# A six-layer cross network on one core: the second half's remainder columns turned by VectorE, one block of products moved, x0 read in twelve pieces, the last layer opened with narrow matmuls

## The chip, the cores and the metric

The kernel runs on one NeuronCore of a Trainium2 chip. TensorE multiplies matrices (its result goes to PSUM, eight banks), ScalarE evicts PSUM and adds biases, VectorE multiplies and adds elementwise, POOL (GpSimd) makes small copies, and SP issues DMA transfers; ScalarE's queue can issue transfers too. Every engine works through its own queue in order and waits on semaphores. The metric is the device time of one execution in microseconds (us); the median of three runs counts.

## The reference

```python
B, F, D, L = 4096, 26, 16, 6
Din = min(F * D, 1024)          # 416
x0: [4096, 416]   ws: [6, 416, 416]   bs: [6, 416]      # all bf16

def reference(x0, ws, bs):
    x = x0
    for l in range(ws.shape[0]):
        x = x0 * (x @ ws[l] + bs[l]) + x
    return x
```

Each layer is a product with a 416 x 416 matrix, a bias, a product with the input x0 and a sum with the layer's own input.

## The kernel before

**Layout.** For layers 0 to 4 the activations lie transposed: features on the partitions, rows of the batch as columns. 416 features are three full blocks of 128 (`NK = 3`, tiles `XM`) and a remainder of 32 (`R`, tiles `XR`). The 4096 rows are two halves `s` of 2048, each of four groups `g` of 512 (`CW`). The remainder of one half is packed: group `g`'s 32 features lie on partitions 32g to 32g+31, so `XR` holds 512 columns for each half. `XM[0]`, `XR[0]` are x0; the layers write `XM[1]`, `XM[2]` by turns. `XRd` is x0's remainder with the upper and lower 64 partitions exchanged.

**Loading (lines 92 to 125).** SP's queue issues eight transposing transfers that bring x0's full blocks, one for each half and group (L75), and between the fifth and the sixth the second half's remainder, `load_xrem1` (L84); then the weights of layer 1 (L71), the remainder rows of the weights (L90), the other layers' weights, x0 row by row in four transfers (`X0rows`, L123; only the last layer reads it) and the last bias (L125). ScalarE's queue issues the first layer's weights, the biases, the first half's remainder in four transfers into `xrig` (`load_xrem0`, L80) and the first layer's remainder rows, and then copies the latter to other partitions (L108). POOL fills a block-diagonal copy of the remainder weights (`fill_wd`, L129) and, between, rearranges `xrem` into `xrig[:, 1]` (L132).

**The first layer (`first_layer`, called for both halves).** Full-width products (L212) go into PSUM tiles of two banks, the remainder's row products (L219) are row-tiled: four matmuls of 32 rows side by side in the array. `x0_rem(s, tpr)` turns x0's remainder: four TensorE transposes (L155) into PSUM, then three VectorE copies (L158), one to `XR[0]` and two to `XRd`. For `s = 0` it stands in the middle of the first products; for `s = 1` at the end of the first half, behind the remainder products `mm_rem` (L191 and L196, column-tiled: 32 columns of the array for each group) and ahead of the second block's elementwise work. `ew_main` is that work for 1024 columns: ScalarE adds the bias out of PSUM (L163), VectorE multiplies by x0 (L164) and adds the layer's input (L167). PSUM is one pool of four two-bank tiles, taken by turns: a new tile waits until ScalarE has emptied the oldest. The buffers `t` between ScalarE and VectorE are six.

**Layers 1 to 4 (lines 280 to 311).** Six tiles (half, block) in three pairs `n = 0, 2, 4`. In each pair, tile a gets its full products in column-tiled form (`mm_full`, L179: four matmuls of 32 columns side by side) and then its row products (L185), tile b its row products and then its full ones. Behind the first pair, `rem_pair` computes both halves' remainder products (L191, L196), their eviction (L171) and their elementwise work (L172, L173). These write the remainder that the next layer reads in its row products. In layer 4 the results also go, by transposing transfers, to `XLrows` (L203).

**The last layer (lines 313 to 380).** Its output has batch rows on the partitions: weights are the activations, 128 columns of them at a time, and the moving side is the weight matrix, 416 wide. Four rounds of eight banks each. `mm_q_full` (L325) makes three full-width matmuls for one bank; in each round `done` banks open with them (two in the first round), then `mm_q_rem` adds the remainder (L331) and the bias (L334) by row-tiled matmuls, and the others close with them. ScalarE copies out of PSUM (L352), VectorE multiplies by `X0rows` (L353) and adds `XLrows` (L342), and SP stores (L343).

**Order.** A planner orders each engine's queue by estimated times, within the data's dependences; an instruction handed to `keep_in_program_order` stays where the program has it among its engine's instructions. Transfers get one of eight semaphores each, by turns in the planner's order.

Of the kernel before, what the change touches and what calls it, by code (L numbers as in the profile page):

```python
# [11 lines left out]
BF16 = mybir.dt.bfloat16  # L12
# [4 lines left out]
def kernel(  # L17
# [7 lines left out]
    nc = tc.nc  # L25
    B, D = x0.shape
    L = ws.shape[0]
    P = 128
    NK = 3
    R = D - NK * P  # L30
    assert R == 32 and B == 4096 and D == 416 and L >= 2
    NS = 2
    NG = 4
    CW = 512
    SW = NG * CW
    NBT = B // P
# [3 lines left out]
    big = ctx.enter_context(tc.tile_pool(name="big", bufs=1))  # L40
# [4 lines left out]
    x0_v = x0.rearrange("(bt p) d -> p bt d", p=P)  # L45
    out_v = out.rearrange("(bt p) d -> p bt d", p=P)

    ident = const.tile([P, P], BF16)
    dz = const.tile([P, 2], FP32)
    ones = const.tile([P, P], BF16)  # L50
    WM = const.tile([P, L, NK, D], BF16)
# [6 lines left out]
    X0rows = big.tile([P, NBT, D], BF16)  # L58
    XLrows = big.tile([P, NBT, D], BF16)
    scrR = [big.tile([P, 4, P], BF16, name=f"scrR{s}") for s in range(NS)]  # L60
    xrem = big.tile([P, 16, R], BF16)
    xrig = big.tile([P, NS, 4, P], BF16)
    XRd = big.tile([P, NS * CW], BF16)
    XM = [big.tile([P, NK, B], BF16, name=f"XM{i}") for i in range(3)]
    XR = [big.tile([P, NS * CW], BF16, name=f"XR{i}") for i in range(3)]

    def col0(s, g):
        return SW * s + CW * g

    def load_wm(eng, l):  # L70
        eng.dma_start(WM[:, l], ws[l, 0:NK * P, :].rearrange("(k p) n -> p k n", p=P))  # L71

    def load_x0t(s, g):
        c0 = col0(s, g)
        nc.sync.dma_start_transpose(out=XM[0][:, :, c0:c0 + CW], in_=x0[c0:c0 + CW, 0:NK * P])  # L75

    def load_xrem0():
        with nc.allow_non_contiguous_dma(reason="64B row segments"):
            for i in range(4):
                nc.scalar.dma_start(xrig[:, 0, i, :].rearrange("p (g r) -> p g r", g=NG), x0_v[:, i:16:4, NK * P:D])  # L80

    def load_xrem1():
        with nc.allow_non_contiguous_dma(reason="64B row segments"):
            nc.sync.dma_start(xrem[:], x0_v[:, 16:32, NK * P:D])  # L84

    def load_wr0():
        nc.scalar.dma_start(WR[0:R, 0, :], ws[0, NK * P:D, :])
# [17 lines left out]
    for g in range(1, NG):  # L105
        dst, src = WR[32 * g:32 * g + 32, 0, :], WR[0:R, 0, :]
# [4 lines left out]
    for g in range(2, NG):  # L111
        load_x0t(0, g)
    load_x0t(1, 0)
    load_xrem1()
    for g in range(1, NG):
        load_x0t(1, g)
    load_wm(nc.sync, 1)
# [1 line left out]
        load_wr(nc.sync, g, 1, L)  # L119
    for l in range(2, L):  # L120
        load_wm(nc.sync, l)
    for q in range(4):
        nc.sync.dma_start(X0rows[:, 8 * q:8 * q + 8, :], x0_v[:, 8 * q:8 * q + 8, :])  # L123
    for g in range(NG):
        nc.sync.dma_start(bLr[32 * g:32 * g + 1, :], bs[LL:LL + 1, :])  # L125

    def fill_wd(l0, l1):
        for g in range(NG):
            nc.gpsimd.tensor_copy(WD[32 * g:32 * g + 32, l0:l1, g, :], WR[32 * g:32 * g + 32, l0:l1, NK * P:D])  # L129

    fill_wd(0, 1)
    nc.gpsimd.tensor_copy(xrig[:, 1].rearrange("p i (g r) -> p i g r", g=NG), xrem[:].rearrange("p (g i) r -> p i g r", g=NG))  # L132
    fill_wd(1, L)

    wps = psum.tile([P, CW], FP32, tag="ps", name="wps")
# [14 lines left out]
        nc.vector.tensor_copy(bM[:], pb[:, 0:NK, 0:L])  # L150
        nc.vector.tensor_copy(bR[:], pb[:, 3, 0:L])

    def x0_rem(s, tpr):
        for i in range(4):
            nc.tensor.transpose(tpr[:, 128 * i:128 * i + 128], xrig[:, s, i, :], ident[:])  # L155
        for dst, src in ((slice(0, P), slice(0, P)), (slice(64, P), slice(0, 64)), (slice(0, 64), slice(64, P))):
            to = XR[0] if dst == src else XRd
            nc.vector.tensor_copy(to[dst, CW * s:CW * s + CW], tpr[src])  # L158

    def ew_main(l, s, m, h, pt, cur, nxt, pin=False):  # L160
        c0 = col0(s, 2 * h)
# [37 lines left out]
    def new_pts():  # L199
        return [psum.tile([P, 2, CW], FP32, tag="ps", name=f"pt{h}") for h in range(2)]  # L200

    def xl_dmat(s, k, nxt):
        nc.sync.dma_start_transpose(out=XLrows[:, 16 * s:16 * s + 16, 128 * k:128 * k + 128],  # L203
                                    in_=nxt[:, k, SW * s:SW * s + SW])

    def first_layer(s):
        cur, curR, nxt, nxtR = XM[0], XR[0], XM[1], XR[1]

        def full(pt, m, h, gl, after_row):
            c0 = col0(s, 2 * h + gl)  # L210
            for k in range(NK):
                nc.tensor.matmul(pt[:, gl, :], lhsT=WM[:, 0, k, 128 * m:128 * m + 128], rhs=cur[:, k, c0:c0 + CW],  # L212
                                 start=(k == 0 and not after_row), stop=(k == NK - 1 and after_row))

        def row(pt, m, h, opens):
            for gl in range(2):
                rg = 32 * ((2 * h + gl) ^ (2 if m == 1 else 0))
                src = XRd if m == 1 else curR
                nc.tensor.matmul(pt[:, gl, :], lhsT=WR[rg:rg + 32, 0, 128 * m:128 * m + 128],  # L219
                                 rhs=src[rg:rg + 32, CW * s:CW * s + CW],  # L220
                                 start=opens, stop=not opens, tile_position=(rg, 0))

        def ph(m):
            return psum.tile([P, 2, CW], FP32, tag="ps", name=f"ph{m}")

        pa = [ph(m) for m in range(NK)]
        if s == 0:
            for m in range(NK):
                full(pa[m], m, 0, 0, False)
            tp0 = psum.tile([P, CW], BF16, tag="ps", name="tpr")  # L230
            x0_rem(0, tp0[:])
            for m in range(NK):
                full(pa[m], m, 0, 1, False)
        else:
            for m in range(NK):
                for gl in range(2):
                    full(pa[m], m, 0, gl, False)
        pb = [ph(0)]
        row(pa[0], 0, 0, False)
        row(pb[0], 0, 1, True)  # L240
        row(pa[2], 2, 0, False)
        row(pa[1], 1, 0, False)
        for m in range(NK):
            ew_main(0, s, m, 0, pa[m], cur, nxt)
        for m in range(NK):
            if m:
                pb.append(ph(m))
            for gl in range(2):
                full(pb[m], m, 1, gl, m == 0)
        row(pb[1], 1, 1, False)  # L250
        row(pb[2], 2, 1, False)
        pr = psum.tile([P, 2, CW], FP32, tag="ps", name="pr")
        mm_rem(0, s, pr[:, 0, :], cur, curR)
        if s == 0:
            x0_rem(1, pr[:, 1, :].bitcast(BF16)[:, 0:CW])
        for m in range(NK):
            ew_main(0, s, m, 1, pb[m], cur, nxt, pin=(s == 0))
        ew_rem(0, s, pr[:, 0, :], curR, nxtR)
# [20 lines left out]
    cur, curR = XM[1], XR[1]  # L279
    for l in range(1, LL):  # L280
        nxt, nxtR = XM[1 + (l % 2)], XR[1 + (l % 2)]
        feeds_last = (l == LL - 1)
        tiles = [(s, m) for s in range(NS) for m in range(NK)]
        pts = {}

        def finish(t):
            s, m = t
            for h in range(2):
                ew_main(l, s, m, h, pts[t][h], cur, nxt)
            if feeds_last:  # L290
                xl_dmat(s, m, nxt)

        for n in range(0, len(tiles), 2):
            ta, tb = tiles[n], tiles[n + 1]
            pts[ta] = new_pts()
            for g in range(NG):
                mm_full(l, ta[0], ta[1], g, pts[ta], cur, True, False)
            mm_row(l, ta[0], ta[1], pts[ta], curR, False, True)
            pts[tb] = new_pts()
            mm_row(l, tb[0], tb[1], pts[tb], curR, True, False)  # L300
            if feeds_last and n == 4:
                xl_rem(0)
            finish(ta)
            for g in range(NG):
                mm_full(l, tb[0], tb[1], g, pts[tb], cur, False, True)
            finish(tb)
            if n == 0:
                rem_pair(l, cur, curR, nxtR, feeds_last)
        if feeds_last:
            xl_rem(1)  # L310
        cur, curR = nxt, nxtR

    l = LL
# [4 lines left out]
    def q_cols(q, g):  # L318
        s, i = quads[q]
        c = col0(s, g) + 128 * i  # L320
        return slice(c, c + 128)

    def mm_q_full(q, g, py, closes):
        for k in range(NK):
            nc.tensor.matmul(py[:, 0:D], lhsT=cur[:, k, q_cols(q, g)], rhs=WM[:, l, k, :],  # L325
                             start=((not closes) and k == 0), stop=(closes and k == NK - 1))
# [34 lines left out]
    for q, at, done in rounds:  # L361
        tiles = [psum.tile([P, 2, CW], FP32, tag="ps", name=f"py{n}") for n in range(4)]
        bank = [tiles[n][:, a, :] for n, a in at]

        def close(u, n):
            tl, a = at[u]
            ew(q + u // 4, u % 4, n, tiles[tl][:, a:a + n, 0:D], nc.scalar if q + 2 == NQ and u == 7 else nc.sync)

        for u in range(done):
            mm_q_full(q, u, bank[u], False)  # L370
        mm_q_rem(q, bank[0:4], done)
        close(0, done)
        mm_q_rem(q + 1, bank[4:8], 0)
        for u in range(done, 8):
            mm_q_full(q + u // 4, u % 4, bank[u], True)
            if at is not PAIRS:
                close(u, 1)
            elif u % 2:
                close(u - 1, 2)
# [31 lines left out]
```

## Time and profile before

| | us |
|---|---|
| runs (median of 3; lowest to highest) | 130.45; 130.38 to 130.53 |
| the profiled execution | 130.58 |
| its span, first to last instruction | 128.8 |
| granted TensorE clock | 1.00 |

| Stretch of the span, us | what runs | TensorE busy | VectorE busy | ScalarE busy |
|---|---|---|---|---|
| 0 to 5.9 | first loads | 5.13 | 0.06 | 0.00 |
| 5.9 to 26.8 | first layer | 20.90 | 15.31 | 14.70 |
| 26.8 to 46.1 | layer 1 | 19.30 | 18.42 | 14.24 |
| 46.1 to 65.4 | layer 2 | 19.30 | 17.39 | 13.72 |
| 65.4 to 84.6 | layer 3 | 19.20 | 17.29 | 13.62 |
| 84.6 to 103.7 | layer 4 | 19.10 | 17.20 | 14.14 |
| 103.7 to 115.7 | last layer, up to the last round's remainder | 12.00 | 10.95 | 8.55 |
| 115.7 to 128.8 | end | 8.71 | 10.06 | 7.91 |

A line of the profile names the line of the kernel (L212 is line 212), the engine (PE is TensorE's matmuls, PEld its weight loads, DVE is VectorE, ACT ScalarE; ACTq and SPq are the sequencers), the operation, and the tiles as out<-in. In the chain of waits the columns are start, duration and what ran; in the timeline they are start, duration and the instruction with its count, and in brackets the engine's idle time before it and what ended that.

### The profile page before, as it was taken

The numbers are of one execution on the slowest core, as the hardware profiler recorded it, in microseconds if no ns is written. First come the engines' busy times: TensorE is split into PE (matmuls) and PEld (weight loads), VectorE is DVE, ScalarE is ACT, GpSimd is POOL, SyncE is SP. The second block draws the span as 40 slices with busy tenths as digits, with TensorE's granted clock in tenths as the row PEclk, the third lists the DMA queues.
The fourth block names the chain that finished last, engine by engine and source line by source line (L and its number), as shares of the span: only waits on it lengthen the run. The fifth ranks groups of instructions, "written<-read, shape, count | busy, mean of one in ns | idle before, by whom it ended". The sixth has DMA issues, their size and how long they took to land.

```text
span 128.8 us, 3973 instructions
## 1 busy us (share of the span) xinstructions
PE 123.6 (96%) x1691; PEld 55.1 (43%) x1691; DVE 106.7 (83%) x195; ACT 86.9 (67%) x99; POOL 6.2 (5%) x18
## 2 busy tenths in 40 slices
PE   7999999999999999999999999999999999999960
PEld 3343443344545444434444544444444445445420
DVE  0023989999999898989898989898989899898991
ACT  0138873887848667848668848668858896569670
POOL 4004300600000000000000000000000000000000
PEclk9999999999999999999999999999999999999999
DMA  4999999999990000000000000000297999985754
GB/s 95 244 231 207 163 153 264 253 328 333 336 291 9 5 0 8 0 0 5 0 5 0 5 0 5 0 5 0 45 163 169 119 237 191 217 261 186 235 178 138
DMA packets 42102, 16.37 MB, mean 127 GB/s; under 512 B 30906, under 2 KB 42084, under 8 KB 42084
## 3 DMA queue, kind: packets, MB, share of 16 engines
q1 hardware_dynamic: 39368, 15.53, 53.9%
q10 hardware_dynamic: 2716, 0.59, 2.5%
q8 instruction: 13, 0.21, 0.7%
q14 instruction: 5, 0.04, 0.1%
HBM read 6.15 MB, written 3.41 MB: 74 GB/s over the span
## 4 chain that ended last, share of the span: by engine, by line
PE 89%; DVE 6%; issue 2%; ACT 1%; DVEq 0%
PE pt L179 49%; PE ph L212 13%; PE py L325 8%; PE pt L185 5%; PE pr L196 5%; PE wps L139 4%; DVE t L353 4%; DVE o L342 2%; PE pr L191 2%; PE ph L219 1%; PE py L331 1%; PE py L334 1%; ACT t L352 1%; PE tpr L155 0%; PE pr L155 0%
## 5 line engine op out<-in xcount | busy, mean ns | idle before, releaser
L179 PE MATMUL pt<-XM,WM 128*32 128x512 bf16 x1152 | 65.2, 379 | 0.0
L163 ACT ACTIVATE t<-pt,bM 128x1024 bf16<-128x1024 f32 x48 | 49.6, 1115 | 18.5 <-PE pt L185 18.5
L164 DVE TENSOR_TENSOR t<-t,XM 128x1024 bf16<-128x1024 bf16 x60 | 41.4, 690 | 5.2 <-ACT t L163 5.2
L167 DVE TENSOR_TENSOR XM<-t,XM 128x1024 bf16<-128x1024 bf16 x60 | 41.8, 697 | 3.4
L179 PEld LDWEIGHTS <-WM 128*32 128x32 bf16 x1152 | 29.7, 97 | 33.8 <-issue 5.1
L352 ACT CAST t<-py 128x416 bf16<-128x416 f32 (+1 forms) x23 | 14.8, 642 | 4.8 <-PE py L325 2.6
L325 PE MATMUL py<-WM,XM 128*128 128x416 bf16 x96 | 17.7, 340 | 0.0
L212 PE MATMUL ph<-XM,WM 128*128 128x512 bf16 x72 | 16.5, 381 | 0.0
L163 ACT ACTIVATE t<-ph,bM 128x1024 bf16<-128x1024 f32 x12 | 12.5, 1114 | 3.4 <-PE ph L219 3.4
L325 PEld LDWEIGHTS <-XM 128*128 128x128 bf16 x96 | 9.0, 98 | 8.5 <-issue 1.4
L353 DVE TENSOR_TENSOR t<-t,X0rows 128x416 bf16<-128x416 bf16 (+1 forms) x23 | 10.4, 457 | 1.2 <-ACT t L352 1.2
L342 DVE TENSOR_TENSOR o<-t,XLrows 128x416 bf16<-128x416 bf16 (+1 forms) x23 | 10.4, 456 | 0.0
L212 PEld LDWEIGHTS <-WM 128*128 128x128 bf16 x72 | 6.7, 98 | 8.4 <-issue 1.1
L171 ACT ACTIVATE t<-pr,bR 128x512 bf16<-128x512 f32 x10 | 6.4, 685 | 2.7 <-PE pr L196 2.1
L196 PE MATMUL pr<-XM,WM 128*32 128x512 bf16 x120 | 8.2, 379 | 0.0
L185 PE MATMUL pt<-XR,WR 32*128 32x512 bf16 x96 | 7.3, 379 | 0.0
L139 PE MATMUL wps<-const-bfloat16-1.0 128*128 128x512 bf16 (+1 forms) x12 | 4.9, 592 | 0.8 <-PEq L395 0.8
L104 ACT ACT_TABLE_LOAD x1 | 1.3, 1283 | 6.0 <-DMA XM<-in_x_dram 6.0
L173 DVE TENSOR_TENSOR XR<-t,XR 128x512 bf16<-128x512 bf16 x10 | 4.2, 425 | 0.7
L196 PEld LDWEIGHTS <-WM 128*32 128x32 bf16 x120 | 3.2, 97 | 3.0
L150 DVE CAST bM<-pb 128x18 f32<-128x18 bf16 x1 | 0.2, 177 | 5.1 <-PE pb L149 5.1
L172 DVE TENSOR_TENSOR t<-t,XR 128x512 bf16<-128x512 bf16 x10 | 4.2, 420 | 0.0
(38 smaller groups left out, 33.5 us busy)
## 6 DMA issues: line engine op xcount, KB each, us to landing
X0rows<-in_x_dram SPq DMA_DIRECT2D x4, 832.0 KB, 11.5
out_dram<-o SPq DMA_DIRECT2D x9, 208.0 KB, 2.5
WM<-in_ws_dram SPq DMA_DIRECT2D x5, 312.0 KB
out_dram<-o SPq DMA_DIRECT2D x13, 104.0 KB, 1.9
WR<-in_ws_dram SPq DMA_DIRECT2D x4, 130.0 KB, 4.1
WM<-in_ws_dram ACTq DMA_DIRECT2D x1, 312.0 KB
XM<-in_x_dram SPq DMA_TRANSPOSE x8, 4.9
xrig<-in_x_dram ACTq DMA_DIRECT2D x4, 32.0 KB, 4.2
```

Source lines behind the costliest of these rows:

```text
L139: nc.tensor.matmul(wps[:, 0:cols], lhsT=warm[:, 0:P], rhs=warm[:, 0:cols], start=True, stop=True)
L163: nc.scalar.activation(t[:], pt[:].rearrange("p a b -> p (a b)"), ACT.Identity, bias=bM[:, m, l:l + 1], scale=1.0)
L164: prod = nc.vector.tensor_tensor(out=t[:], in0=t[:], in1=XM[0][:, m, c0:c0 + 2 * CW], op=ALU.mult)
L167: nc.vector.tensor_tensor(out=nxt[:, m, c0:c0 + 2 * CW], in0=t[:], in1=cur[:, m, c0:c0 + 2 * CW], op=ALU.add)
L179: nc.tensor.matmul(pts[g // 2][32 * q:32 * q + 32, g % 2, :], lhsT=WM[:, l, k, 128 * m + 32 * q:128 * m + 32 * q + 32], rhs=cur[:, k, c0:c ...
L185: nc.tensor.matmul(pts[g // 2][:, g % 2, :], lhsT=WR[32 * g:32 * g + 32, l, 128 * m:128 * m + 128], rhs=curR[32 * g:32 * g + 32, CW * s:CW ...
L196: nc.tensor.matmul(pr[32 * g:32 * g + 32, :], lhsT=WM[:, l, k, NK * P:D], rhs=cur[:, k, c0:c0 + CW], start=False, stop=(k == NK - 1), tile ...
L212: nc.tensor.matmul(pt[:, gl, :], lhsT=WM[:, 0, k, 128 * m:128 * m + 128], rhs=cur[:, k, c0:c0 + CW], start=(k == 0 and not after_row), sto ...
L325: nc.tensor.matmul(py[:, 0:D], lhsT=cur[:, k, q_cols(q, g)], rhs=WM[:, l, k, :], start=((not closes) and k == 0), stop=(closes and k == NK ...
L342: tc.keep_in_program_order(nc.vector.tensor_tensor(out=o, in0=t, in1=xl, op=ALU.add))
L352: nc.scalar.copy(tv, src)
L353: tc.keep_in_program_order(nc.vector.tensor_tensor(out=tv, in0=tv, in1=X0rows[:, b, :], op=ALU.mult))
```

## The change

Four edits:

- **The second half's remainder.** `x0_rem` becomes `x0_rem0` (first half, as before) and `x0_rem1`. The transfer of `xrem` moves from SP's queue, between x0's groups, to ScalarE's, behind a one-column `memset` of the same tile on VectorE, both in program order directly behind the three copies of `x0_rem0`. It reads other rows: partition p now holds rows 16p to 16p+15 of the second half instead of every 128th. `x0_rem1` is one VectorE transpose of 32 x 32 blocks from `xrem` to `XR[0]`, its output interleaved with a step of 16, and two VectorE copies from `XR[0]` to `XRd`. The four TensorE transposes, the three copies out of PSUM and POOL's rearranging copy are gone for this half.
- **Layer two's remainder products.** In the layer with `l == 1`, `rem_pair` stands behind the pair `n == 2` (blocks three and four) instead of `n == 0`; the other layers keep it.
- **x0's rows.** The four transfers of eight row blocks become twelve of two or three.
- **The opening of the last layer.** In round `q == 0` the two opening banks are computed by `mm_q_open`: 128 x 32 weights and `tile_position=(0, j)`, four matmuls for each full-width one.

```diff
-    xrig = big.tile([P, NS, 4, P], BF16)
+    xrig = big.tile([P, 4, P], BF16)
...
+    def pin(ins):
+        tc.keep_in_program_order(ins)
+
...
     def load_xrem1():
+        pin(nc.vector.memset(xrem[:, 0, 0:1], 0.0))
         with nc.allow_non_contiguous_dma(reason="64B row segments"):
-            nc.sync.dma_start(xrem[:], x0_v[:, 16:32, NK * P:D])
+            pin(nc.scalar.dma_start(xrem[:], x0[SW:2 * SW, NK * P:D].rearrange("(p t) r -> p t r", p=P)))
...
     load_x0t(1, 0)
-    load_xrem1()
     for g in range(1, NG):
...
-    for q in range(4):
-        nc.sync.dma_start(X0rows[:, 8 * q:8 * q + 8, :], x0_v[:, 8 * q:8 * q + 8, :])
+    for q in range(12):
+        b0, b1 = NBT * q // 12, NBT * (q + 1) // 12
+        nc.sync.dma_start(X0rows[:, b0:b1, :], x0_v[:, b0:b1, :])
...
     fill_wd(0, 1)
-    nc.gpsimd.tensor_copy(xrig[:, 1].rearrange("p i (g r) -> p i g r", g=NG), xrem[:].rearrange("p (g i) r -> p i g r", g=NG))
     fill_wd(1, L)
...
-    def x0_rem(s, tpr):
+    def x0_rem0(tpr):
         for i in range(4):
-            nc.tensor.transpose(tpr[:, 128 * i:128 * i + 128], xrig[:, s, i, :], ident[:])
+            nc.tensor.transpose(tpr[:, 128 * i:128 * i + 128], xrig[:, i, :], ident[:])
         for dst, src in ((slice(0, P), slice(0, P)), (slice(64, P), slice(0, 64)), (slice(0, 64), slice(64, P))):
             to = XR[0] if dst == src else XRd
-            nc.vector.tensor_copy(to[dst, CW * s:CW * s + CW], tpr[src])
+            pin(nc.vector.tensor_copy(to[dst, 0:CW], tpr[src]))
+        load_xrem1()
+
+    def x0_rem1():
+        pin(nc.vector.transpose(XR[0][:, CW:2 * CW].rearrange("p (j t) -> p t j", t=16), xrem[:]))
+        for dst, src in ((slice(64, P), slice(0, 64)), (slice(0, 64), slice(64, P))):
+            pin(nc.vector.tensor_copy(XRd[dst, CW:2 * CW], XR[0][src, CW:2 * CW]))
...
-            x0_rem(0, tp0[:])
+            x0_rem0(tp0[:])
...
         if s == 0:
-            x0_rem(1, pr[:, 1, :].bitcast(BF16)[:, 0:CW])
+            x0_rem1()
...
-            if n == 0:
+            if n == (2 if l == 1 else 0):
                 rem_pair(l, cur, curR, nxtR, feeds_last)
...
+    def mm_q_open(q, g, py):
+        c = q_cols(q, g).start
+        for k in range(NK):
+            for j in range(0, P, 32):
+                nc.tensor.matmul(py[j:j + 32, 0:D], lhsT=cur[:, k, c + j:c + j + 32], rhs=WM[:, l, k, :],
+                                 start=(k == 0), stop=False, tile_position=(0, j))
...
         for u in range(done):
-            mm_q_full(q, u, bank[u], False)
+            if q == 0:
+                mm_q_open(q, u, bank[u])
+            else:
+                mm_q_full(q, u, bank[u], False)
```

More of the change, by code (lines that the diff above doesn't have):

```diff
@@ L79, in load_xrem0 @@
             for i in range(4):
-                nc.scalar.dma_start(xrig[:, 0, i, :].rearrange("p (g r) -> p g r", g=NG), x0_v[:, i:16:4, NK * P:D])
+                nc.scalar.dma_start(xrig[:, i, :].rearrange("p (g r) -> p g r", g=NG), x0_v[:, i:16:4, NK * P:D])
     def load_xrem1():
+        pin(nc.vector.memset(xrem[:, 0, 0:1], 0.0))
         with nc.allow_non_contiguous_dma(reason="64B row segments"):
-            nc.sync.dma_start(xrem[:], x0_v[:, 16:32, NK * P:D])
+            pin(nc.scalar.dma_start(xrem[:], x0[SW:2 * SW, NK * P:D].rearrange("(p t) r -> p t r", p=P)))
     def load_wr0():
```

## The prediction

> **What bounds the kernel now.** I read the totals of the engines first, then the chain of waits in order of time, then the waits by engine, then the timeline around each edited place.
>
> ```profile
> PE 123.6 (96%) x1691; PEld 55.1 (43%) x1691; DVE 106.7 (83%) x195; ACT 86.9 (67%) x99; POOL 6.2 (5%) x18
> ```
>
> TensorE is busy for 96% of the 128.8 us span. That alone decides nothing; the chain does:
>
> ```profile
> 15.41 0.33 PE ph L219 x4
> 15.73 0.33 PE pr L191 x4
> 16.06 0.65 PE pr L196 x12
> 16.71 0.33 PE pr L155 x4
> 17.04 3.88 PE ph L212 x18
> 20.93 0.54 PE ph L219 x8
> 21.47 3.99 PE ph L212 x18
> ...
> 29.36 0.54 PE pt L185 x8
> 29.90 2.71 PE pt L179 x48
> 32.60 0.21 PE pr L191 x4
> 32.82 0.65 PE pr L196 x12
> 33.47 0.22 PE pr L191 x4
> 33.68 0.65 PE pr L196 x12
> 34.33 2.59 PE pt L179 x48
> ...
> 101.01 2.70 PE pt L179 x48
> 103.71 1.16 PE py L325 x6
> 104.87 0.29 PE py L331 x4
> ...
> 110.84 4.33 PE py L325 x24
> ...
> 115.65 0.02 issue
> 115.67 0.86 ACT t L352
> ```
>
> Each line starts where the one before ended: from 8.40 to 115.65 us TensorE runs without a hole, and then one eviction by ScalarE and 9.6 us of VectorE products and sums end the kernel. In the waits by engine, TensorE waits only at its very start (0.8 us). So a matmul taken out before 115.65 shortens the kernel by its own time, as long as nothing else becomes late; and VectorE, ScalarE and the DMAs count only where they hold TensorE or lie in the last ten microseconds.
>
> **A price that recurs: changing the tile shape.** The 48 matmuls of L179 take 2.59 us behind the column-tiled L196 but 2.70 behind the row-tiled L185. A change of shape costs 0.11 us.
>
> **Part by part.** First the work taken off TensorE. The four transposes of L155 go: 0.33 us. They stand between column-tiled L196 and full-width L212, and carry that change of shape; it now falls on the next line, which goes from 3.88 to about 3.99, as behind L219. Gain 0.33 - 0.11 = **0.22 us**.
>
> The last layer's opening is 6 full-width matmuls in 1.16 us. Without a change of shape the same line runs at (4.33 - 0.11) / 24 = 0.176 each, so 6 take 1.05. The change makes 24 matmuls of 128x32 of them, directly behind the column-tiled L179. Four 512-wide ones of that shape take 2.59 / 12 = 0.216 us; scaled to 416 columns that is the 0.176 of one full-width matmul. So 1.05 us, and the change of shape ahead disappears (the one ahead of L331 stays). Gain **0.11 us**. This scaling is what I choose; the other bound is no scaling at all, 24 x 0.054 = 1.30 us, a loss of 0.14. The spacing can go below that: four 32-column matmuls of 6 columns (L149) take 0.12 us, 0.03 each.
>
> The remainder products of layer two (32.60 to 34.33, 1.73 us) move behind the next two blocks. Both places lie between L179 groups of the same shape: **0**. Their results (VectorE 36.79 to 38.47 now) come one pair of blocks later, 2.59 + 0.54 + 2.70 = 5.8 us, at about 44.3; layer three's first row products read them at 48.59. In exchange, the second half's layer-one output, done at 31.55, is first read at 33.47 now, and after the move by the row products of block four, at about 35.3 (32.38 + 2.59 + 0.27). The cover grows from 1.9 to 3.7 us.
>
> Now VectorE. Removed are three PSUM copies (0.42 + 0.86 = 1.28 us at 17.08); added are a one-column memset, one 32x32-block transpose of 128x512, and two 64x512 copies inside SBUF. No row shows the transpose: the nearest are the 0.42 us VectorE copy of that size and POOL's rearranging copy (1.06 us, L132). I take 0.69, half the two-operand rate, worked out from rows: 512 more elements cost 0.27 us there (0.42 at 128x512, 0.69 at 128x1024). The copies: between 0.15 (the fixed part of those rows) and 0.42; I take 0.42, the L158 row. Sum 0.06 + 0.69 + 0.84 = 1.59, between 0.78 and 1.96, against 1.28: from 0.5 less to 0.7 more. POOL's copy is gone, and with it the stretch of the VectorE sum at 15.62, 0.98 instead of 0.69. All of this stands against 3.7 us of cover: **0**.
>
> The transpose waits for xrem. Today that transfer is triggered by SP at 10.31 and lands at 14.88. Afterwards ScalarE's queue triggers it behind VectorE's memset, at about 10.1, so by the same 4.6 us it lands near 14.7, and VectorE gets there at 15.62 + 0.69 = 16.3. Everything on VectorE is queued behind it; up to 3.7 us late costs nothing, beyond that TensorE waits one for one.
>
> The trigger itself stands in ScalarE's queue ahead of its first eviction (L163 at 11.09):
>
> ```profile
> 9.66 1.10 ACT L108 COPY WR<-WR 32x416 bf16<-32x416 bf16 x2 [2.07 <-DMA WR<-in_ws_dram]
> 11.09 4.13 ACT L163 ACTIVATE t<-ph,bM 128x1024 bf16<-128x1024 f32 x4 [0.33 <-PE ph L219]
> ```
>
> The nearest trigger is L84's on SP, same segments, 0.58 us. L163's semaphore wait was taken at 9.67, when the first copy had only begun, so the sequencer runs ahead and the trigger lies under the copies: 10.1 to 10.7, and the eviction starts with its data as now. If it ran behind the copies it would end at 11.34, the eviction at 12.46. TensorE needs that PSUM tile back for block m = 1 at 11.42 + 6 x 0.222 = 12.75. So **0**, until the trigger ends later than 12.75 - 1.11 = 11.6. The longest trigger of any kind here took 3.08 (a transposing one); at that it would cost 10.76 + 3.08 - 11.6 = 2.2 us.
>
> SP loses a 0.58 us trigger, so three transposed loads start about 0.6 us earlier. Group (1,1) landed at 16.96 and is read at 17.68 now, 17.46 then; the same bytes go ahead of it as now. **0**.
>
> x0's rows: 12 triggers instead of 4 on SP, the same 3.4 MB; they land by about 40 us (40.17 now), VectorE first reads them at 107.43, and SP has nothing else from 34.5 to 91. bLr behind them has until 105. VectorE gets up to eight more semaphore waits (17 such at L342, 21 ns in the median). Where one stands now, at 116.57, product to sum still takes 0.51 us, as without it. **0**; if none of the eight hid, 0.17.
>
> **The sum:** 0.22 + 0.11 = 0.33 us. The profiled execution took 130.58 us around its span of 128.8; it becomes 130.25 (span 128.5). The runs' median is 130.45 (130.38 to 130.53), so **130.12**.
>
> **Rivals.**
>
> *The trigger waits for an earlier transfer (slower).* The transfers use eight semaphores in turn. In this trace the fourth xrig trigger started at 4.01, where the first weights' transfer on the same semaphore landed at 3.99: a trigger waits for the one eight places before it. Now that wait stands in ScalarE's queue. It costs nothing while the older transfer has landed by 11.0 (11.6 - 0.58), which holds for all xrig loads (8.36 at the latest) and the third x0 group (9.83). If the planner numbers xrem behind more of SP's triggers, it gets the semaphore of group (1,0), landed at 13.53: trigger to 14.1, eviction to 15.2, TensorE 2.5 us late, 130.12 + 2.5 = **132.6**. With group (0,3), 11.15, it is 0.2: 130.3. For it: the numbering isn't shown. Against: it needs some seven SP triggers ahead, and SP reached its sixth only at 10.95.
>
> *xrem itself is late (slower).* If it lands with the last x0 group (21.16), TensorE's row products at 20.71 wait until 21.16 + 1.53 = 22.7: **132.1**. Against: a landing of 4.6 us now, 4.2 for xrig.
>
> *The narrow opening gets slower.* Without scaling: -0.22 + 0.14, so **130.37**. [...]
>
> *The tail keeps part.* VectorE runs close-packed from 116.55 on; if the extra waits all show there, 130.12 + 0.17 = **130.29**.
>
> **How the numbers follow.** Forecast 0.55; opening unscaled 0.10; tail 0.10; trigger wait 0.17, of which 0.05 for its mild form; late xrem 0.05; weight loads 0.03. Two runs of this kernel can be told apart from about 0.2%, 0.26 us, that is below 130.19 or above 130.71. Of the forecast's 0.55 (own range 130.0 to 130.25) I count 0.52 as faster and 0.03 as same; same also gets the opening, the tail and the mild wait, 0.28 in all; slower is 0.12 + 0.05 + 0.03 = 0.20. The range starts at 129.95 (the full 0.33 of L155 plus 0.11, less the runs' spread of 0.07) and reaches to 131.4, which leaves out the strong wait and the late xrem, 0.17.
>
> **What would show it.** L212 behind L196 at 3.99 and starting at 16.71; the opening at 1.05; no new hole in the chain before 115.3; ScalarE's first eviction still at 11.1; VectorE's transpose at 16 to 17 us, 0.4 to 1.1 long; L179 following L179 at 32.4. A wait of ScalarE before L163, or of TensorE between 12 and 23 us, would prove the forecast wrong.

## The result, and the profile after

| | before | after |
|---|---|---|
| median of 13 runs each, us | 130.52 (130.38 to 130.82) | 130.18 (130.10 to 130.74) |
| ratio, 95% interval | | 0.9975 (0.9966 to 0.9984) |
| span of the profiled execution, us | 128.805 | 128.396 |

The change is 0.25% faster. 130.12 had been forecast against a median of 130.45, which is the same ratio, 0.9975. The interval's upper end is a gain of 0.16%, just inside what I had called no difference. Single executions at a granted clock of about 0.66, which take some 184 us, are left out of all ratios below.

The totals of the engines after:

```profile
PE 122.6 (96%) x1705; PEld 55.1 (43%) x1705; DVE 108.1 (84%) x196; ACT 86.7 (68%) x99; POOL 4.6 (4%) x17
```

TensorE does one microsecond less (123.6 before), VectorE 1.4 more (106.7), POOL 1.6 less. The chain of waits of the kernel after, in order of time (start, duration, what ran):

```profile
15.36 0.33 PE ph L228 x4
...
16.02 0.65 PE pr L205 x12
16.66 3.99 PE ph L221 x18
20.66 0.54 PE ph L228 x8
...
29.63 5.29 PE pt L188 x96
...
103.44 1.05 PE py L336 x24
104.50 0.29 PE py L347 x4
```

L221 (L212 before) follows the column-tiled L205 directly and takes 3.99 instead of 3.88. Between 29.63 and 34.92 there are 96 products in one piece: the remainder products no longer stand there. The opening takes 1.05. Compared with the chain before, the line at 15.36 starts 0.05 earlier (15.41; the first weights' remainder rows happened to land at 9.59 instead of 9.64), the full products 0.38 earlier (16.66 against 17.04), the row products 0.27 (20.66 against 20.93) and the line behind the opening 0.37 (104.50 against 104.87). VectorE's last sum ends 0.38 us earlier, at 125.81 instead of 126.19, and the span is 0.41 shorter.

VectorE's timeline around the new transpose (start, duration, instruction):

```profile
15.65 0.69 DVE L176 TENSOR_TENSOR XM<-t,XM 128x1024 bf16<-128x1024 bf16 x1
16.26 2.36 DVE L165 STREAM_TRANSPOSE XR<-xrem 128x512 bf16<-128x512 bf16 x1
18.66 0.61 DVE L167 COPY XRd<-XR 64x512 bf16<-64x512 bf16 x2
19.29 0.69 DVE L173 TENSOR_TENSOR t<-t,XM 128x1024 bf16<-128x1024 bf16 x1
```

The transpose takes 2.36 us, far outside my bounds of 0.42 and 1.06. With its copies and the memset `x0_rem1` costs VectorE 3.03 us, against 1.28 before, and the next product starts at 19.29 instead of 18.31. Nothing of it reaches TensorE's chain above.

ScalarE's timeline at the same place:

```profile
10.07 0.62 ACTq L88 DMA_DIRECT2D xrem<-in_x_dram  x1
10.17 0.54 ACT L112 COPY WR<-WR 32x416 bf16<-32x416 bf16 x1
11.12 3.12 ACT L172 ACTIVATE t<-ph,bM 128x1024 bf16<-128x1024 f32 x3 [0.41 <-PE ph L228]
```

The trigger runs under a copy of the same engine, as assumed, and the eviction starts at 11.12 (11.09 before). `xrem` lands at 16.18, 6.1 us behind its trigger and not 4.6, but VectorE reaches the transpose only at 16.26.

### The profile page after: what moved, and what is told of

It is laid out like the page before. It is cut to its first block, busy times and chain, and to the rows that moved or that the text cites. A ratio compares the mean times of both kernels' runs of the same rounds, so it can differ in the third digit from the quotient of the medians.

```text
span 128.4 us, 4012 instructions
## 1 busy us (share of the span) xinstructions
PE 122.6 (96%) x1705; PEld 55.1 (43%) x1705; DVE 108.1 (84%) x196; ACT 86.7 (68%) x99; POOL 4.6 (4%) x17
## 4 chain that ended last, share of the span: by engine, by line
PE 81%; DVE 7%; DMA 6%; ACTq 2%; issue 1%; ACT 1%; DVEq 0%
PE pt L188 49%; PE ph L221 11%; PE pt L194 5%; PE pr L205 5%; DVE t L369 4%; PE py L341 4%; DMA xrig<-in_x_dram 4%; DVE o L358 3%; DMA out_dram<-o 2%; PE pr L200 2%; PE ph L228 1%; PE py L336 1%; ACTq L83 1%; PE py L347 1%; ACT t L368 1%
## 5 line engine op out<-in xcount | busy, mean ns | idle before, releaser
L221 PE MATMUL ph<-XM,WM 128*128 128x512 bf16 x72 | 16.4, 379 | 0.3 <-DMA XM<-in_x_dram 0.3
L341 PE MATMUL py<-WM,XM 128*128 128x416 bf16 x90 | 16.5, 339 | 0.0
L341 PEld LDWEIGHTS <-XM 128*128 128x128 bf16 x90 | 8.5, 98 | 7.8 <-issue 1.4
L221 PEld LDWEIGHTS <-WM 128*128 128x128 bf16 x72 | 6.8, 98 | 9.0 <-issue 1.6
L205 PE MATMUL pr<-XM,WM 128*32 128x512 bf16 x120 | 8.2, 379 | 0.0
L142 PE MATMUL wps<-const-bfloat16-1.0 128*128 128x512 bf16 (+1 forms) x12 | 4.3, 544 | 0.8 <-PEq L414 0.8
L182 DVE TENSOR_TENSOR XR<-t,XR 128x512 bf16<-128x512 bf16 x10 | 4.4, 435 | 0.6
L205 PEld LDWEIGHTS <-WM 128*32 128x32 bf16 x120 | 3.2, 97 | 3.0
```

Source lines behind the costliest of these rows:

```text
L205: nc.tensor.matmul(pr[32 * g:32 * g + 32, :], lhsT=WM[:, l, k, NK * P:D], rhs=cur[:, k, c0:c0 + CW], start=False, stop=(k == NK - 1), tile ...
```

## The experiments

Ratios are against the kernel before, run on the same chip, with 95% intervals. Its medians in the four comparisons were 130.53, 130.53, 130.56 and 130.54.

### The two terms of the sum

The opening alone, in the kernel before:

```diff
-            mm_q_full(q, u, bank[u], False)
+            (mm_q_open(q, u, bank[u]) if q == 0 else mm_q_full(q, u, bank[u], False))
```

> The kernel before with the column-tiled opening alone. Theory (the gain is the sum of two stretches taken off TensorE's chain, each worth its own time): the opening takes 1.05 us instead of 1.16 and the whole is 0.11 us faster than before, ratio about 0.9992. Rival (the gain comes from elsewhere, or the two parts need each other): no difference, or the whole 0.34.

Measured: 130.46, ratio 0.9993 (0.9984 to 1.0002). The changed kernel without the opening:

```diff
-            if q == 0:
+            if False:
```

> The changed kernel with the last layer opened by full-width matmuls as before. Theory: the opening takes 1.16 us again, the line behind the remainder products 3.99 without transposes ahead of it; 0.22 us faster than before, 0.11 slower than the change, ratio about 0.9983. Rival: it keeps the whole gain, or loses it.

Measured: 130.35, ratio 0.9986 (0.9978 to 0.9995). The two gains, 0.07 and 0.14%, add up to 0.21 of the 0.25%, within their intervals. Each is near its term (0.11 and 0.22 us, that is 0.08 and 0.17%); the opening alone can't be told from nothing by its times, only by its 1.05 us in the chain.

### What covers the long transpose

The changed kernel with layer two's remainder products back behind the first pair:

```diff
-            if n == (2 if l == 1 else 0):
+            if n == 0:
```

> The changed kernel with layer two's remainder products left behind block two. Theory (the move only buys cover): TensorE would read the second half's first-layer remainder at about 33.2 us, and VectorE had it ready at 32.95 in the changed kernel, so 0.25 us of cover is left and the time is that of the change, ratio 0.9975. Rival (the move was needed against the long transpose): TensorE waits at 33.2 and the gain shrinks by the wait, 0.1 to 0.5 us.

Measured: 130.29 (130.13 to 130.95), ratio 0.9990 (0.9978 to 1.0002). The move is worth 0.1 us by the medians and 0.2 us by the ratios, where I had expected nothing; the intervals of the two kernels overlap. Two of the twelve runs took 130.9. One of those was profiled: `xrem` landed at 17.00 instead of 16.18, and TensorE waited 0.3 us for the remainder (L200 for L182) at 33.4. Another 0.7 us of that execution is a wait for a group of x0 in the first layer, which the move does not touch.

Since one transpose fits under its cover, the cover is measured by adding to it: one or two more transposes of the same shape into a tile that nobody reads.

```diff
+        for _ in range(1):
+            pin(nc.vector.transpose(xtwice[:].rearrange("p (j t) -> p t j", t=16), xrem[:]))
```

> The changed kernel with VectorE's transpose made a second time, into a tile that nobody reads: 2.36 us more on VectorE. Theory (cover): the second half's first-layer remainder is ready at 32.95 + 2.4 = 35.3 us, TensorE reads it in block four's row products at about 35.2; the time grows by 0.1 us or not at all over the change. Rival (VectorE is nearly saturated, so all added work shows at the end): 2.4 us slower than the change, ratio about 1.016.

> The changed kernel with the transpose made three times in all, 4.7 us more on VectorE. Theory (cover of 2.2 us left in the changed kernel, then one for one): TensorE waits about 2.5 us in front of block four's row products or earlier for PSUM that ScalarE cannot empty for want of buffers; 2.5 us slower than the change, ratio about 1.017. Rival (all hidden): no change. Rival (all shows): 4.7 us slower.

> The same second transpose, with layer two's remainder products left behind block two. Theory (cover): they read the second half's remainder at 33.2 us and get it at 35.3, so TensorE stands still for about 2.1 us there; some 2.1 us slower than the change, ratio about 1.014. Rival (the move buys nothing): the same time as with the products moved.

Measured: two transposes 1.0020 (1.0010 to 1.0029), three 1.0195 (1.0175 to 1.0216), two without the move 1.0133 (1.0115 to 1.0151). The figure for three rests on two runs, 133.08 and 133.14; a third took 135.12 at a mean granted clock of 0.987, which the next section comes back to. An added transpose is 2.2 to 2.4 us in the chain of the last of the three. The first costs 0.6 us against the changed kernel (130.84 less 130.18) and not the 0.1 that I had expected, so about 1.6 us of cover were left; both together cost 0.0220 x 130.5 = 2.9 of some 4.5 us, which leaves 1.6 again. Taking the move away, with two transposes, costs another 1.5 us. TensorE's timeline of the kernel with two transposes and no move shows both places that wait, the first of them:

```profile
20.70 0.60 PE L231 MATMUL ph<-XR,WR 32*128 32x512 bf16 x6
21.67 0.39 PE L231 MATMUL ph<-XRd,WR 32*128 32x512 bf16 x2 [0.37 <-DVE XRd L170]
```

and its waits by engine the second (us in total, times, longest):

```profile
PE pr L203 <- DVE XR L185: 1.5, 1, 1.5
```

So there are two readers. The added transposes stand behind the one that writes `XR[0]` and ahead of the copies to `XRd`, so at the first reader they delay `XRd` alone. The row products of the second half's first block (L228 after, L231 here) read `XRd` from 20.82 on in the kernel after, where its two copies end at 18.97 and 19.27: 1.6 us, as measured. The remainder behind it, ready at 32.95, is read by block four's row products at about 35.2 with the move and by the products L200 at 33.4 without it. The move widens the second cover alone.

Why the transpose is long: its output has a step of 16 elements. With a dense output,

```diff
-        pin(nc.vector.transpose(XR[0][:, CW:2 * CW].rearrange("p (j t) -> p t j", t=16), xrem[:]))
+        pin(nc.vector.transpose(XR[0][:, CW:2 * CW].rearrange("p (t j) -> p t j", t=16), xrem[:]))
```

> The changed kernel with the transpose's output written densely, not with a step of 16 columns; the second half's remainder columns come out in another order, so the output is not the reference's there. Theory A (the step of 16 in the output makes the transpose 2.36 us): it falls to 0.6 or 0.7 us. Theory B (a 32x32-block transpose of 512 bf16 columns costs that whatever the output's step): it stays near 2.36. The whole kernel's time is that of the change in both cases, since VectorE has cover there.

Measured: 130.21, ratio 0.9977 (0.9965 to 0.9989), as the changed kernel. VectorE's timeline of this kernel:

```profile
16.30 0.70 DVE L165 STREAM_TRANSPOSE XR<-xrem 128x512 bf16<-128x512 bf16 x1
17.04 0.61 DVE L167 COPY XRd<-XR 64x512 bf16<-64x512 bf16 x2
```

0.70 us: my 0.69 was right for a dense output, and the step makes 2.36 of it. No run here has a step between 1 and 16. The 1.66 us saved leave the time as it was, so they lay under cover.

### The trigger of xrem

Behind a group that lands late: the memset is replaced by a copy of one column out of x0's group (1,0), so that `xrem`'s trigger, in ScalarE's queue, waits for that transfer.

```diff
-        pin(nc.vector.memset(xrem[:, 0, 0:1], 0.0))
+        pin(nc.vector.tensor_copy(xrem[:, 0, 0:1], XM[0][:, 0, SW:SW + 1]))
```

> The changed kernel with the memset ahead of xrem's transfer replaced by a one-column copy out of x0's group (1,0), so that ScalarE's trigger waits for that group's landing (13.2 us). Theory (what stands in ScalarE's queue behind the trigger is the first eviction, and TensorE needs its PSUM tile at 12.75): trigger 13.3 to 13.9, eviction ready at about 15.0, TensorE 2.3 us late, 2.3 us slower than the change, about 132.5 us. Rival (the wait is hidden, since TensorE has other tiles to fill): no change.

Measured: 133.93 (132.99 to 134.81), ratio 1.0257 (1.0191 to 1.0323). The four runs fall in two: 133.0 and 133.2 at a mean granted clock of 0.998, 134.6 and 134.8 at 0.984 to 0.986. The chain of waits of one of the latter:

```profile
13.57 0.62 ACTq L88
...
14.24 1.12 ACT t L172
15.36 0.04 issue
15.40 4.16 PE ph L221 x12
```

Trigger, eviction, TensorE 2.71 us late: this is the chain that the prediction's first rival priced at 2.5 us, forced here by the copy. But the twelve products behind the wait take 4.16 us, where twelve take 2.66 elsewhere (18 in 3.99). A table of windows over that place shows why (start and end of the window, its length, busy time and count of each engine, then the granted clock):

```profile
17.00:20.00 3.00, 3.00 (x10) 0.72 (x8) 2.39 (x4) 1.37 (x2) 0.00 (x0) 0.50 1.31 215
20.00:24.00 4.00, 4.00 (x34) 1.73 (x31) 3.87 (x5) 2.70 (x3) 1.37 (x3) 1.00 1.16 247
```

The granted clock is 0.50 from 17 to 20 us and 1.00 from there: in this execution a stall of 2.7 us cost 1.5 more (4.16 less 2.66). Here the halved clock followed an idle time of 2.71 us. Behind TensorE's wait of 1.46 us in the kernel with two transposes and no move, and behind the 0.84 us of the early trigger below, the granted clock stays at 1.00. That it fell in the second of the two longer runs, and in the run of 135.12 us with three transposes, is read from their mean granted clocks alone (0.984 and 0.987).

With no memset the trigger goes out as early as it can, ahead of ScalarE's first table load:

```diff
-        pin(nc.vector.memset(xrem[:, 0, 0:1], 0.0))
...
     load_wr0()
+    load_xrem1()
     nc.scalar.activation(dz[:, 1:2], dz[:, 0:1], ACT.Identity, bias=dz[:, 0:1], scale=1.0)
...
-        load_xrem1()
```

> The changed kernel without the memset, xrem's transfer triggered on ScalarE's queue at about 6 us, behind the first weights' remainder rows. Theory (the memset keeps 2048 short segments out of the way of x0's groups): group (0,3), landed at 11.23 and read at 12.0, and group (0,2) come later by up to xrem's own 1.4 us; TensorE waits 0 to 0.7 us in the first layer, ratio to before 0.998 to 1.003. Rival (the transfers share without harm): the time of the change, and VectorE's transpose starts no later.

Measured: 131.58, ratio 1.0073 (1.0055 to 1.0091), beyond the range of the theory. TensorE's timeline of this kernel:

```profile
13.50 3.40 PE L219 MATMUL ph<-XM,WM 128*128 128x512 bf16 x15 [0.84 <-DMA XM<-in_x_dram]
```

The group waited for is (0,3). It lands at 13.46, in the kernel after at 11.28. The sharing of the DMA engines, which the theory named, can be only the smaller part of that. The waits of SP's queue by engine (us in total, times, longest) have a row that the kernel after lacks:

```profile
SPq L75 <- DMA XM<-in_x_dram: 1.8, 1, 1.8
```

`xrem` is now numbered ahead of (0,3) and takes the semaphore that (0,3) had. (0,3) gets the next one, that of (0,1), and SP holds its trigger until (0,1) has landed at 8.76: it goes out at 8.78 instead of 6.78. So 2.0 of the 2.2 us are the numbering, the mechanism of the prediction's first rival in SP's queue instead of ScalarE's. Another group comes later as well: (0,2) lands at 11.32 instead of 9.79, with its trigger only 0.26 us later, but it is not read before 11.84. The row products ahead end 0.5 us later because the remainder rows of the first weights land at 10.13 instead of 9.59; half of that was there at their trigger, ahead of `xrem`'s.

The memset does no arithmetic that is needed, but it holds the transfer back, and the kernel without it is 1.4 us slower than the changed one. How much would be left if (0,3) had kept its semaphore is not shown.

### Twelve loads or four

The term that I had put at nothing, undone alone:

```diff
-    for q in range(12):
-        b0, b1 = NBT * q // 12, NBT * (q + 1) // 12
+    for q in range(4):
+        b0, b1 = NBT * q // 4, NBT * (q + 1) // 4
```

> The changed kernel with x0's rows in four transfers as before. Theory: the number of transfers is covered in both forms, the time is that of the change, ratio 0.9975. Rival: twelve transfers shorten or lengthen something (the queue behind them, VectorE's waits in the last layer), up to 0.17 us either way.

Measured: 130.55, ratio 1.0003 (0.9994 to 1.0011). The whole gain is gone. TensorE and VectorE run as in the changed kernel, VectorE even ends 0.03 us earlier (125.78 against 125.81), but the span is 128.85 instead of 128.40: the stores end later. In each kernel one of SP's 22 store triggers of the last layer (one more is ScalarE's) comes late although its data is ready. Two neighbours from SP's timeline, store 14 and 15 of the kernel after:

```profile
120.94 0.33 SPq L359 DMA_DIRECT2D out_dram<-o  x1
...
121.80 0.33 SPq L359 DMA_DIRECT2D out_dram<-o  x1
```

and store 18 and 19 with four loads:

```profile
123.24 0.33 SPq L359 DMA_DIRECT2D out_dram<-o  x1
...
124.09 0.33 SPq L359 DMA_DIRECT2D out_dram<-o  x1
```

0.85 us lie between these triggers, 0.57 between others. In the kernel before the late one is store 18 (123.08, then 123.91). After a late one SP follows at 0.43 to 0.47 each until it has caught up, some three stores later. With four loads there are only three left, one of them takes 0.71, and the last trigger, 0.28 late at 125.80, falls together with ScalarE's at 125.81. Its store lands at 127.96; in the kernel after the last to land is ScalarE's, at 127.57. That is 0.40 of the 0.46 us between the two spans.

Two theories: the late trigger stands at a fixed number of SP's own instructions, or the size of the pieces matters. Eight small loads more, with x0's rows still in four:

```diff
+    for k in range(8):
+        nc.sync.dma_start(bLr[k + 1:k + 2, :], bs[LL:LL + 1, :])
```

> The changed kernel with x0's rows in four loads, as in the run with four loads (1.0003 there), and eight more small transfers on SP behind the loads of the last bias: the bias row once more into eight rows of bLr that nobody reads. SP has then as many instructions ahead of the stores as in the changed kernel (105 in its trace against 97 with four loads). Theory (SP's queue stops for about 0.8 us at a fixed number of its own instructions, and with four loads this stop falls between stores 18 and 19, too late to be made up): the stop is back between stores 14 and 15, span 128.4, ratio 0.9975. Rival (the size of the pieces of x0's rows matters, or when they land): 1.0003 as before, about 130.55 us.

Measured: 130.22, ratio 0.9971 (0.9960 to 0.9982). SP's timeline, store 14 and 15:

```profile
120.84 0.33 SPq L361 DMA_DIRECT2D out_dram<-o  x1
...
121.70 0.33 SPq L361 DMA_DIRECT2D out_dram<-o  x1
```

And the kernel before with one load fewer:

```diff
-    for q in range(4):
-        nc.sync.dma_start(X0rows[:, 8 * q:8 * q + 8, :], x0_v[:, 8 * q:8 * q + 8, :])
+    for q in range(3):
+        b0, b1 = NBT * q // 3, NBT * (q + 1) // 3
+        nc.sync.dma_start(X0rows[:, b0:b1, :], x0_v[:, b0:b1, :])
```

> The kernel before with x0's rows in three loads instead of four, nothing else: one instruction fewer on SP ahead of the stores. In the kernel before, SP's stop stands between the wait ahead of store 18 and that store (123.45 to 123.91). Theory: it moves on by one instruction, to behind store 18 and ahead of the wait of store 19, as with four loads in the changed kernel; the last three triggers then come some 0.3 us late and fall together with ScalarE's store: 0.35 us slower, ratio 1.0027, about 130.9 us. Rival (the size of the pieces matters): three pieces against four is nearly the same, within 0.1 us of before, ratio 1.000.

Measured: 130.66, ratio 1.0014 (1.0005 to 1.0023). SP's timeline, store 18 and 19:

```profile
123.78 0.33 SPq L344 DMA_DIRECT2D out_dram<-o  x1
...
124.64 0.33 SPq L344 DMA_DIRECT2D out_dram<-o  x1
```

The stop moves by count, both times to the store foretold, and the sizes of the pieces don't matter. Other profiles at the full clock agree: six more kernels with twelve loads have the late trigger at store 15, among them the one with the late trigger of `xrem`, where every store is some 4 us later; the kernel before with the opening alone has it at store 18.

The price of the stop in the last kernel is not what I expected. By the ratio this kernel is 0.18 us slower, half of the 0.35, and even that can't all be put down to the stop: in the profiled execution the products that follow the transposes of `x0_rem` start at 17.18 instead of 17.04, so 0.14 of the 0.21 us between the two spans is there long before the stores, and 0.07 arises behind VectorE's last sum. No later trigger took 0.71, and store 22 was on time again. So the place of the stop alone does not set its price.

What the stop is, is not shown. In the five kernels of this section a packet of 8,192 bytes on the DMA queue of kind "instruction" starts about 0.6 us after the late instruction (at 122.38 behind 121.80 in the kernel after, at 124.55 behind 123.91 in the kernel before). Such packets also start where no trigger of SP is late (at 124.53 in the kernel after), so they prove nothing. The stop takes some 0.4 us: in the kernel after, SP's next instruction starts 0.45 us behind the end of the trigger of 120.94, and 0.05 us behind most others. It is hidden there and worth 0.37 us with four loads.

## Why the prediction held, and where it didn't

**The sum.** The transposes' 0.22 and the opening's 0.11 were right in the chain, including the change of shape that L221 takes over (3.99) and the opening at 1.05 that scales with its columns. 0.33 was forecast, 0.37 to 0.38 is the difference at both ends, of which 0.05 was there before the first edit.

**The transpose** was mis-sized: 0.69 became 2.36. "No row shows the transpose" was true, but I bounded it by rows with dense outputs although the diff shows a step of 16. The sum of `x0_rem1`, 1.59 with a bound of 1.96, is 3.03.

**Its cover** was too wide in my text. I set all of it against the 3.7 us ahead of block four's row products; the row products of the second half's first block, at 20.7, which I used only in the rival of a late `xrem`, stand nearer. With my sizes 2.9 us would have been left there (20.71 less 16.3 and 1.53). Measured, 1.6 are left. The **0** came out right because even 3.03 us fit, and the move kept the second cover from being the narrower one.

**The twelve loads at 0** are the step that failed, in its reason: "SP has nothing else from 34.5 to 91" looks at when the loads run, not at what they do to the position of everything behind them in SP's queue. They are worth 0.0028 x 130.5 = 0.37 us, as much as the sum. They hide a cost that the sum lacked as well: the trigger taken from SP, also put at **0**, moves the late store from 18 to 19. In the changed kernel the two cancel. That the total came out right is luck in this part: with four loads the same sum would have been forecast, and nothing would have been gained.

**The trigger under ScalarE's copies** held: no delay. The semaphore taken in turn was that of the fourth `xrig` load, landed at 8.39, so the rival did not come; the late trigger shows its price, 2.5 forecast and 2.7 in TensorE's wait, without the clock behind it. The early trigger shows that a new number can also make SP's own triggers wait, which I had not considered. For the milder form I took (0,3) as landed at 11.15; the last completion is at 11.51, so it would have cost 0.5 us and not 0.2. A late `xrem` happens in a mild form (16.2 to 17.0). The opening lost nothing, so its unscaled form did not show. No run shows weight loads that hide under nothing, the term behind the 0.03 and the 131.4 at which the range ends: in the kernel after, the opening's 24 loads of 97 ns, 2.33 us in sum, run beside its products, and the whole takes 1.05 us. The aside on L149 misreads the chain: 0.12 us is what remained behind L147, and the four matmuls take 0.19, side by side from 5.72 to 5.91. The tail kept nothing: from the last product to the end VectorE runs as before.

## What to carry to other kernels

A sum over the chain of waits was good to a few hundredths here, where every moved cost was covered; so look for the nearest reader of each late result, not the one that the edit is about, and for steps in the access pattern before taking a duration from a dense row. Instructions added to or removed from a queue move everything behind them: where a kernel ends in a row of stores from one queue, compare the intervals between their triggers in both traces before believing that an edit elsewhere on that queue is free. A transfer that changes its place can also change the semaphores of those numbered behind it, so look for a trigger that waits. When a result is right, undo each part that was priced at nothing: two that were wrong may have cancelled.

## What the hardware showed unexpectedly

- SP stopped for some 0.4 us at a fixed number of its own instructions, with its data ready (0.45 us between two instructions in the kernel after, 0.05 elsewhere): one instruction fewer moved the stop by one store, eight more by four (a store is a wait and a trigger).
- VectorE's transpose of 128x512 bf16 took 0.70 us with a dense output and 2.36 with a step of 16 elements.
- A stall of TensorE of 2.71 us was followed by a granted clock of 0.50 until 20 us, 1.5 us lost beyond the stall; of four runs, two have a lower mean clock (0.984 and 0.986 against 0.998).
- 128 KB in 64-byte segments landed 4.6 us after their trigger on SP, and 6.1 to 6.9 us after one on ScalarE's queue at the same time (reading other rows); sent at 6.3 us they landed in 5.3, and a group of x0 sent before them came 1.3 us slower.
- A trigger on SP waited 1.8 us for the transfer eight places before it to land, after a transfer on another engine's queue had taken its semaphore.
